# Attention over pooled keys and two dense layers on one core: the kernel lists its own instructions and orders them

## The chip, the cores and the metric

The kernel runs on one core of a Trainium2 chip. The metric is the device time of one execution in microseconds; the median of 3 runs before the change is 1000.41 us. The engines are TensorE (PE, with its weight loads, PEld), VectorE (DVE), ScalarE (ACT), GpSimd (POOL) and SyncE (SP, which issues most loads). Each engine takes its own instructions strictly in the order in which they were emitted for it, and waits for the others by semaphores.

## The reference

Eight batches of 576 tokens, 8 heads of 64 columns. The keys and values of a head are averaged over windows of 8, so that 72 are left; attention over them gives x of 4608 tokens by 512 columns, and two dense layers follow:

```python
k_p = k.reshape(B, H, 72, 8, 64).mean(axis=3)         # v_p in the same way
scores = np.matmul(q, k_p.transpose(0, 1, 3, 2)) / 8
attn = exp(scores - max); attn = attn / (sum + 1e-9)
x = np.matmul(attn, v_p)                              # to (4608, 512)
h = x @ w_in                                          # (512, 2048)
g = h * (1.0 / (1.0 + np.exp(-1.702 * h)))
out = g @ w_out                                       # (2048, 512)
```

The weights arrive as float64; q, k and v as float32.

## The kernel before

*Products.* An operand of float32 is split into hi, its rounding to 12 bits, and lo, the rest. A product is then three passes of the fast type: hi with hi, hi with lo, lo with hi. Lines 563 to 565 are the passes of `h` (w_in times x), lines 583 to 585 those of `o` (g times w_out). For a chunk of tokens `moe_in` computes h for one block of 128 of the 2048 columns (16 blocks, here called f = 0 to 15; for chunks of 256 tokens two blocks at once), ACT applies the gelu twice (line 569 gives gh, the hi part, 570 gives g), and line 572 subtracts to gl, the lo part, on DVE for the first two chunks and on POOL after that. `moe_out` adds the block to one accumulator of 128 tokens by 512 columns each, and after the last block ACT copies it out (588) and stores it (589). There are three chunks of 256 tokens and ten of 384.

*Weights.* The 33 parts of 512 (at the end 256) columns are turned from float64 to float32 by `decode_weights`: ACT 520 and 522, DVE 527 (shift) and 528 (merge), POOL 532, then ACT 538 writes the hi part and 543 the lo part, on POOL for three parts of four and on DVE for the fourth.

*Attention.* A batch's 576 tokens are two pieces of 256 and 320. Window sums of keys and values are made by `spread`: in the first batch by eight products with an identity on PE (line 142), in the others by a DVE reduction (147). Scores are float32 products (308), which take two instruction records each. DVE takes the maximum off (320, 321), ACT exponentiates (354), DVE sums (359) and multiplies by the inverse. In the first batch the multiply is wide (369), and PE turns the weights, tokens to keys (412). In the others 16 + 8 narrow multiplies a piece (389, 381) lay them out so that DVE can turn blocks of 32 (422, 437). The turned weights are split (ACT 425, DVE 426), multiplied with the values in four passes into `pav` (452 to 455), and split again into x (ACT 458, DVE 459). Pieces that reach over the end of a chunk leave a part in `stage`.

*Order.* `stream` is a generator of attention's stages. The main loop emits the products of one block of one chunk and then pulls stages out of the generator at a pace set by constants (`PACE`, `EARLY`, `DECODED`). The framework then reorders what was emitted, by a timeline simulation of its own (`schedule_with_timeline_sim`). x has two buffers, h two banks of PSUM, o three, attention three.

Of the kernel before, what the change touches and what calls it, by code (L numbers as in the profile page):

```python
# [19 lines left out]


@with_exitstack
def attention_moe_kernel(ctx: ExitStack, tc: tile.TileContext, q, k, v, w_in, w_out, out):
    """Every float32 product is three float32r passes: an operand x is hi + lo, hi the rounding of
    x to 12 significant bits and lo the exact rest, and hi*hi + hi*lo + lo*hi carries float32's bits."""
# [3 lines left out]
    NTOK = B * S  # L29
# [11 lines left out]
    # Tokens of a batch in two pieces, and each piece's tiles of tokens: first token and count.  # L41
# [3 lines left out]
    XBUFS = 2  # L45
    HEAD = 3
    CHUNK = 384
    OVER = 192  # tokens of a piece beyond its first chunk, at most
    AHEAD = 1
    PACE = 5  # L50
    EARLY = 13
    FETCHED = 1
    DECODED = 0.8
    LEAD = 4
    GAP = 2
    # The chunks of tokens of the second part: first token and count.
# [29 lines left out]
    x_tiles = {}  # L86

    def x_tile(c):
        if c not in x_tiles:
            x_tiles[c] = xpool.tile([P, 2, NJ, CHUNK], F32R, tag="x", name=f"x{c}")  # L90
        return x_tiles[c]

    def fetch_main(b, u, src, t=None):
        """Keys 0 to 63 of a pair's two heads in the two halves of the partitions."""
        if t is None:
            t = load.tile([P, NP, 512], F32, tag="kv", name=f"kv{b}_{u}_{src is v}")
        for a in range(2):
            ins = nc.sync.dma_start(
                out=t[a * KM : (a + 1) * KM],
                in_=src[b, UH * u + a : UH * (u + 1) : 2, 0 : KM * POOL].rearrange(  # L100
                    "j (p w) d -> p j (w d)", w=POOL
                ),
            )
            if b:
                tc.keep_in_program_order(ins)
        return t

    def fetch_tail(b, u, tl=None, copies=(v, v, v, k)):
        """The last keys of four heads: three copies of v's, and k's."""
        if tl is None:  # L110
            tl = load.tile([P, 512], F32, tag="tl", name=f"tl{b}_{u}")
        for r, src in enumerate(copies):
            if src is not None:
                nc.sync.dma_start(
                    out=tl[r * TAIL : (r + 1) * TAIL],
                    in_=src[b, UH * u : UH * (u + 1), KM * POOL :].rearrange("h (p w) d -> h p (w d)", w=POOL),
                )
        return tl

    def fetch_q(b, piece, j, place=None):  # L120
# [3 lines left out]
        qr = place  # L124
        if qr is None:
            qr = load.tile([P, PMAX // 32, 32], F32, tag="qr", name=f"qr{b}_{piece}_{j}", bufs=2)
        for a in range(2):
            for e in range(2):
                r = (2 * a + e) * 32
                nc.sync.dma_start(  # L130
                    out=qr[r : r + 32, 0 : npc // 32],
                    in_=q[b, 2 * j + a, o0 : o0 + npc, e * 32 : (e + 1) * 32].rearrange("(c i) d -> i c d", i=32),
                )
        return qr

    def spread(b, raw, bd, nm):
        """The window sums of 64 keys of each head, each pair's two heads on a block diagonal."""
        if b == 0:
            ps = ps_a.tile([P, 512], F32, tag="a", name=f"red{b}_{nm}")
            red = ps[:, 0 : NP * D].rearrange("p (i d) -> p i d", i=NP)  # L140
            for w in range(POOL):
                nc.tensor.matmul(
                    red, lhsT=ident, rhs=raw[:, :, w * D : (w + 1) * D], start=w == 0, stop=w == POOL - 1
                )
        else:
            red = att.tile([P, NP, D], F32, tag="red", name=f"red{b}_{nm}")
            nc.vector.tensor_reduce(  # L147
                out=red, in_=raw.rearrange("p i (w d) -> p i d w", w=POOL), axis=AX.X, op=ALU.add
            )
        nc.vector.tensor_tensor(  # L150
            out=bd,
            in0=red.unsqueeze(2).broadcast_to([P, NP, 2, D]),
            in1=mask2.unsqueeze(1).unsqueeze(3).broadcast_to([P, NP, 2, D]),
            op=ALU.mult,
        )
# [4 lines left out]
    batches = {}  # L160

    def fetch_batch(b):
        m = batches[b] = Batch()
        m.v = []
        m.k = [fetch_main(b, u, k) for u in range(NU)]
        m.tl = [fetch_tail(b, 0)]
        return m

    def fetch_first():
        """The first batch, where x and the last parts of the weights will lie; q as it is."""  # L170
        m = batches[0] = Batch()
        kt, vt = (xpool.tile([P, NU, NP, 512], F32, tag="x", name=f"{n}0") for n in "kv")
        m.k, m.v = [kt[:, u] for u in range(NU)], [vt[:, u] for u in range(NU)]
        tl = const.tile([P, NU, 512], F32, tag=f"w{2 * NF - 4}", name="tl0")
        m.tl = [tl[:, u] for u in range(NU)]
        whole, place = [], None

        def fetch_q_tile(i):
            nonlocal place
            s0, ns = (PIECES[0][1] + PIECES[1][1])[i]  # L180
            if i % 2 == 0:
                place = const.tile([P, 2, H, D], F32, tag=f"w{2 * NF - 1 - i // 2}", name=f"q0_{i // 2}")
            nc.sync.dma_start(out=place[:ns, i % 2], in_=q[0, :, s0 : s0 + ns].rearrange("h s d -> s h d"))  # L183
            whole.append(place[:ns, i % 2])
# [8 lines left out]
            "w": lambda: more_raws(len(raws) + 1),  # L193
# [497 lines left out]
```

## Time and profile before

| | us |
|---|---|
| three runs | 1000.41, 997.27, 1000.79 |
| median | 1000.41 |
| span of the profiled execution | 994.9 |
| PE, DVE, ACT, POOL busy | 939.4, 551.3, 411.9, 266.7 |
| mean granted clock of PE | 0.975 |

The profiled execution has no time of its own beside its span, which runs from the first to the last instruction; the median of the runs is 5.5 us above it. A row of a timeline is: start, length, engine, line, operation, result and operands, and in brackets the idle time before it and what ended that. A product's length includes the tail that overlaps the next product, so the pace is read from one start to the next. A row of groups ends with the count, the sum of busy time, the mean in ns, and the idle time ahead.

### The profile page before, as it was taken

Reading aid. Unit: us, or ns where it says so; the run is one execution under the profiler, and the core shown is the slowest. Engines: PE = TensorE matmul, PEld = TensorE weight load, DVE = VectorE, ACT = ScalarE, POOL = GpSimd, SP = SyncE. Lnnn points to the kernel's source line nnn. Section 1 sums busy time; section 2 is a strip of 40 time slices with the busy share of each in tenths; the row PEclk is TensorE's granted clock in tenths of the full one; section 3 lists DMA queues with packets and bytes.
Section 4 is the critical chain, followed back from the end, with each engine's and each line's share of the span. In section 5 each row is a group of like instructions: output and inputs, shape, how many; then the busy total and the mean of one; then the engine's idle time right before and its main releaser. Section 6 shows DMA issues by size and latency. Waiting matters only on the chain.

```text
span 994.9 us, 13412 instructions
## 1 busy us (share of the span) xinstructions
PE 939.4 (94%) x4957; PEld 835.0 (84%) x4957; DVE 551.3 (55%) x1094; ACT 411.9 (41%) x837; POOL 266.7 (27%) x240
## 2 busy tenths in 40 slices
PE   5597899989999999999989999999999999999998
PEld 4476698888878999899978989889988999999997
DVE  3999995789989660760788560680685410100000
ACT  3788553444336432452434342442445332322222
POOL 2568620111212222222212222222212322222222
PEclk8689799999999999999999999999999999999999
DMA  8984341312233030130223030130010000000000
GB/s 208 340 241 126 74 102 32 77 35 52 71 54 85 32 70 1 43 75 1 60 42 85 32 69 1 38 70 1 33 27 1 33 1 0 33 1 1 33 1 32
DMA packets 100449, 57.50 MB, mean 58 GB/s; under 512 B 75168, under 2 KB 83360, under 8 KB 100384
## 3 DMA queue, kind: packets, MB, share of 16 engines
q1 hardware_dynamic: 95200, 47.21, 19.6%
q10 hardware_dynamic: 5184, 9.44, 2.6%
q8 instruction: 39, 0.64, 0.3%
q14 instruction: 26, 0.21, 0.1%
HBM read 47.19 MB, written 9.44 MB: 57 GB/s over the span
## 4 chain that ended last, share of the span: by engine, by line
PE 63%; DVE 18%; DMA 6%; issue 4%; ACT 4%; SPq 3%; POOL 1%; DVEq 0%; ACTq 0%; POOLq 0%
PE h L565 10%; PE o L585 10%; PE h L564 10%; PE o L583 10%; PE h L563 10%; PE o L584 10%; DVE main L389 7%; DMA qr<-in_q_dram 2%; PE sps L308 2%; DMA tl<-in_v_dram 1%; DMA raw<-in_moe_w_out_dram 1%; SPq L183 1%; DVE al L426 1%; DVE tail L381 1%; DVE red_k L147 1%
## 5 line engine op out<-in xcount | busy, mean ns | idle before, releaser
L572 POOL TENSOR_TENSOR gl<-g,gh 128x384 fp32r<-128x384 f32 (+1 forms) x168 | 176.0, 1047 | 619.1 <-ACT g L570 595.6
L564 PE MATMUL h<-x,w 128*128 128x384 f32 (+1 forms) x832 | 274.0, 329 | 4.1 <-POOL w L543 3.5
L565 PE MATMUL h<-x,w 128*128 128x384 f32 (+1 forms) x832 | 273.5, 329 | 1.4 <-DVE x L459 1.4
L563 PE MATMUL h<-x,w 128*128 128x384 f32 (+1 forms) x832 | 273.6, 329 | 0.5 <-ACT x L458 0.4
L569 ACT ACTIVATE gh<-h 128x384 fp32r<-128x384 f32 (+1 forms) x184 | 93.0, 505 | 337.6 <-PE h L565 333.8
L583 PE MATMUL o<-w,gh 128*128 128x512 f32 x576 | 227.9, 396 | 2.6 <-ACT gh L569 2.5
L584 PE MATMUL o<-w,gh 128*128 128x512 f32 x576 | 227.8, 395 | 0.0
L585 PE MATMUL o<-w,gl 128*128 128x512 f32 x576 | 192.0, 399 | 3.3 <-DVE gl L572 3.0
L564 PEld LDWEIGHTS h<-x,w 128*128 128x128 f32 x832 | 160.2, 193 | 14.0 <-POOL w L543 4.1
L563 PEld LDWEIGHTS h<-x,w 128*128 128x128 f32 x832 | 159.9, 192 | 10.8 <-issue 0.8
L565 PEld LDWEIGHTS h<-x,w 128*128 128x128 f32 x832 | 159.2, 192 | 8.0 <-DVE x L459 1.6
L426 DVE TENSOR_TENSOR al<-mt,ah 128x256 fp32r<-128x256 f32 (+1 forms) x56 | 31.9, 569 | 180.1 <-PE pav L454 142.6
L583 PEld LDWEIGHTS o<-w,gh 128*128 128x128 f32 x576 | 108.7, 189 | 19.6 <-ACT gh L569 3.8
L585 PEld LDWEIGHTS o<-w,gl 128*128 128x128 f32 x576 | 106.2, 189 | 22.4 <-DVE gl L572 3.6
L584 PEld LDWEIGHTS o<-w,gh 128*128 128x128 f32 x576 | 108.8, 189 | 16.5 <-issue 0.4
L389 DVE TENSOR_TENSOR main<-sc,sm 32x256 f32<-32x256 f32 (+1 forms) x224 | 118.5, 529 | 3.2
L570 ACT ACTIVATE g<-h 128x384 f32<-128x384 f32 (+1 forms) x184 | 92.1, 501 | 13.8 <-DVE gl L572 6.9
L459 DVE TENSOR_TENSOR x<-pav,x 128x256 fp32r<-128x256 f32 (+3 forms) x64 | 24.9, 390 | 68.0 <-ACT x L458 67.9
L308 PE MATMUL sps<-k,qt 128*128 128x144 f32 (+1 forms) x320 | 57.6, 305 | 2.8 <-DVE sc L321 2.7
L308 PEld LDWEIGHTS sps<-k,qt 128*128 128x128 f32 (+1 forms) x320 | 45.4, 187 | 10.9 <-DVE sc L321 2.9
L532 POOL TENSOR_TENSOR raw<-raw 128x512 uint32<-128x512 uint32 (+1 forms) x33 | 41.5, 1261 | 40.8 <-DVE raw L528 14.5
L425 ACT CAST ah<-mt 128x256 fp32r<-128x256 f32 (+1 forms) x56 | 24.3, 434 | 52.9 <-DVE mt L422 39.6
(80 smaller groups left out, 891.7 us busy)
## 6 DMA issues: line engine op xcount, KB each, us to landing
out_dram<-osb ACTq DMA_DIRECT2D x36, 256.0 KB
raw<-in_moe_w_in_dram SPq DMA_DIRECT2D x16, 512.0 KB
raw<-in_moe_w_out_dram SPq DMA_DIRECT2D x15, 512.0 KB
kv_False<-in_k_dram SPq DMA_DIRECT2D x28, 256.0 KB
kv_True<-in_v_dram SPq DMA_DIRECT2D x28, 256.0 KB
qr<-in_q_dram SPq DMA_DIRECT2D x112, 40.0 KB
qr<-in_q_dram SPq DMA_DIRECT2D x112, 32.0 KB
tl<-in_v_dram SPq DMA_DIRECT2D x48, 64.0 KB
```

The source lines that it names most:

```text
L308: nc.tensor.matmul(ps[:ns, t * PW : (t + 1) * PW], lhsT=qt[:, s0 - o0 : s0 - o0 + ns], rhs=m.k2[:, j], start=True, stop=True,)
L389: nc.vector.tensor_tensor(out=main[32 * r : 32 * (r + 1), :, cols].rearrange("p j t k -> p t j k"), in0=sc[rows, 0:nt, a::2, 32 * half : 3 ...
L426: nc.vector.tensor_tensor(out=al[:, :npc], in0=pt[:, :npc], in1=ah[:, :npc].bitcast(F32), op=ALU.subtract)
L563: nc.tensor.matmul(o, lhsT=w[:, 0, j], rhs=x[:, 0, j], start=j == 0, stop=False)
L564: nc.tensor.matmul(o, lhsT=w[:, 1, j], rhs=x[:, 0, j], start=False, stop=False)
L565: nc.tensor.matmul(o, lhsT=w[:, 0, j], rhs=x[:, 1, j], start=False, stop=j == NJ - 1)
L569: nc.scalar.activation(out=gh, in_=h, func=AF.Gelu_apprx_sigmoid)
L570: nc.scalar.activation(out=g, in_=h, func=AF.Gelu_apprx_sigmoid)
L572: (nc.vector if c < 2 else nc.gpsimd).tensor_tensor(out=gl, in0=g, in1=gh.bitcast(F32), op=ALU.subtract)
L583: nc.tensor.matmul(o, lhsT=gh[:, i, tok], rhs=w[:, 0], start=f == 0, stop=False)
L584: nc.tensor.matmul(o, lhsT=gh[:, i, tok], rhs=w[:, 1], start=False, stop=False)
L585: nc.tensor.matmul(o, lhsT=gl[:, i, tok], rhs=w[:, 0], start=False, stop=f == NF - 1)
```

## The change

`Plan` is a list of tasks, each with an engine, a duration, a due time, the buffers that it reads and writes, and a function that emits it. `order` walks through time: whenever an engine is free, it takes among the tasks whose inputs are there (a fixed waiting time after the task that made them) and whose buffers have room the one with the earliest due time. The result is emitted task by task, and the framework's reordering is switched off (`manual_schedule`). Durations are linear in the size, with constants per engine; a change of ACT's function table adds 1.28, DVE and POOL at work together take 1.3 and 1.2 times as long, PE 1.5 times in the first 60 us.

With it go other edits. A chunk is now the first 512 tokens of a batch, and the ninth chunk gathers the last 64 tokens of all eight batches, which go through a buffer in DRAM; the first chunk is computed as two halves of 256 tokens, the second two blocks behind the first. The second batch is handled like the first (`TURNED = 2`): window sums, and turns of the attention weights, on PE, with wide multiplies on DVE. Each batch's value product has its lo pass last of the four. gl is on DVE only for the first 12 blocks of chunk 0. o has four banks, attention two. Two of a chunk's four outgoing tiles use the buffer of g, two the other one.

```diff
-    CHUNK = 384
-    AHEAD = 1
-    PACE = 5
+    CHUNK = 512
+    HALF = CHUNK // 2
+    LAG = 2
+    TURNED = 2
...
-    ps_o = ctx.enter_context(tc.tile_pool(name="ps_o", bufs=3, space=PSUM))
+    ps_o = ctx.enter_context(tc.tile_pool(name="ps_o", bufs=4, space=PSUM))
-    ps_a = ctx.enter_context(tc.tile_pool(name="ps_a", bufs=3, space=PSUM))
+    ps_a = ctx.enter_context(tc.tile_pool(name="ps_a", bufs=2, space=PSUM))
...
+    def order(self, log=None):
...
+                for t in ready[e]:
+                    if t.ready <= now + 1e-9 and (best is None or (t.due, t.k) < (best.due, best.k)) and self.room(t):
+                        best = t
...
+        if b < TURNED:
+            red = buf(ps_h if b == 0 else ps_a, [P, 512], F32, "h" if b == 0 else "a", f"red{b}_{nm}")
...
+                nc.tensor.matmul(o, lhsT=m.vt()[:96, j], rhs=at()[:96, :npc], start=False, stop=False)
+                nc.tensor.matmul(o, lhsT=m.vh()[:, j], rhs=al()[:, :npc], start=False, stop=True)
...
+                lambda: nc.sync.dma_start(out=left_dram[:, :, b * LEFT : (b + 1) * LEFT], in_=left()),
...
+        if c == 0 and fs[0] < 12:
+            dve(512, lambda: rest(nc.vector), [g, gh], [gl])
+        else:
+            pool(512, lambda: rest(nc.gpsimd), [g, gh], [gl])
...
+    FIRST, STEP, ROUND = 44.0, 6.0, 96.0
...
-        for what in "w k0 w k1 tk tv q q v0 v1 w w w w w w w w q q q".split():
+        for n, what in enumerate("w k0 k1 tk tv q q v0 v1 w w w w w q w q w q".split()):
...
+    for i in range(NF // 2):
+        dense(0, 0, HALF, (2 * i, 2 * i + 1), acc, FIRST + STEP * 2 * i)
+    for i in range(NF // 2):
+        dense(0, HALF, HALF, (2 * i, 2 * i + 1), acc, FIRST + STEP * (2 * i + LAG))
+    for c in range(1, B + 1):
+        acc = {}
+        for f in range(NF):
+            dense(c, 0, CHUNK, (f,), acc, FIRST + STEP * (NF + LAG) + ROUND * (c - 1) + ROUND * f / NF)
+
+    order = plan.order()
+    with tc.manual_schedule():
+        for t in order:
+            t.emit()
```

How it moves instructions, at three places. A row is the line, the operation, the result and its operands, and the shape; a name such as `sc1_0` is batch and piece, `h0_256_2` chunk, first token and block. First DVE, in the first piece of the second batch, from the sum of the exponentials on. Before:

```order
L359 TENSOR_REDUCE sm1_0_994<-sc1_0_992 128x16
L360 TENSOR_SCALAR sm1_0_994<-sm1_0_994 128x16
L363 RECIPROCAL sm1_0_994<-sm1_0_994 128x16
L381 TENSOR_TENSOR tail1_0_1120<-sc1_0_992,sm1_0_994 32x2x32 x2
L389 TENSOR_TENSOR main1_0_1119<-sc1_0_992,sm1_0_994 32x2x4x32 x4
L381 TENSOR_TENSOR tail1_0_1120<-sc1_0_992,sm1_0_994 32x2x32 x2
L389 TENSOR_TENSOR main1_0_1119<-sc1_0_992,sm1_0_994 32x2x4x32 x4
```

and two more such pairs. Now, with decoding of the last weights and the lo parts of the first chunk behind it:

```order
L554 TENSOR_REDUCE sm1_0_1345<-sc1_0_1237 128x16
L566 TENSOR_SCALAR sm1_0_1345<-sm1_0_1345 128x16
L569 RECIPROCAL sm1_0_1345<-sm1_0_1345 128x16
L582 TENSOR_TENSOR tail1_0_1378<-sc1_0_1237,sm1_0_1345 128x128
L582 TENSOR_TENSOR main1_0_1386<-sc1_0_1237,sm1_0_1345 128x1024
L452 TENSOR_TENSOR vl1_1399<-vbd1_1284,vh1_1347 128x512
L873 TENSOR_TENSOR w0_15_1357<-raws_681,w0_15_1357 128x512
```

Twenty-four multiplies became two, and the turns that followed on DVE are gone from it. Second, PE where the first dense products begin. Before, two blocks in turn while the first piece's values are still being made:

```order
L455 MATMUL pav0_0_0_471<-at0_0_0_454,vt0_426 128x256
L412 MATMUL apt0_0_1_490<-ident_79,main0_0_358 128x128 x2
L563 MATMUL h0_0_598<-x0_476,w0_0_177 128x256
L564 MATMUL h0_0_598<-x0_476,w0_0_177 128x256
L563 MATMUL h0_2_837<-x0_476,w0_2_237 128x256
L564 MATMUL h0_2_837<-x0_476,w0_2_237 128x256
L565 MATMUL h0_0_598<-x0_476,w0_0_177 128x256
```

Now, there, the three passes of one block:

```order
L717 MATMUL pav0_0_1_390<-al0_0_1_371,vh0_263 128x256
L639 MATMUL apt0_0_2_400<-ident_79,main0_0_315 128x128 x2
L639 MATMUL apt0_0_3_405<-ident_79,main0_0_315 128x128 x2
L509 MATMUL sps0_1_2_410<-k20_167,qt0_1_2_386 128x144 x2
L509 MATMUL sps0_1_2_410<-k20_167,qt0_1_2_386 64x144
L893 MATMUL h0_0_0_422<-x0_397,w0_0_128 128x256
L894 MATMUL h0_0_0_422<-x0_397,w0_0_128 128x256
L895 MATMUL h0_0_0_422<-x0_397,w0_0_128 128x256
L714 MATMUL pav0_0_2_429<-ah0_0_2_408,vh0_263 128x256
```

And the place further on at which the second half of the tokens (`h0_256_0`) starts, between the last value products of the second piece and the first half's block 5:

```order
L895 MATMUL h0_256_0_686<-x0_397,w0_0_128 128x256
L639 MATMUL apt0_1_3_699<-ident_79,main0_1_563 128x128 x2
L639 MATMUL apt0_1_3_699<-ident_79,main0_1_563 128x64
L714 MATMUL pav0_1_2_706<-ah0_1_2_679,vh0_263 128x320
L715 MATMUL pav0_1_2_706<-ah0_1_2_679,vl0_273 128x320
L716 MATMUL pav0_1_2_706<-at0_1_1_583,vt0_158 128x320
L717 MATMUL pav0_1_2_706<-al0_1_2_691,vh0_263 128x320
L893 MATMUL h0_256_0_686<-x0_397,w0_0_128 128x256
L894 MATMUL h0_256_0_686<-x0_397,w0_0_128 128x256
L895 MATMUL h0_256_0_686<-x0_397,w0_0_128 128x256
L893 MATMUL h0_0_4_577<-x0_397,w0_5_683 128x256
```

Every product of one block stands with its three passes together, both halves of the first 512 tokens use a block's weights shortly after each other, and the lo pass of `pav` has moved from third to last. Third, ACT at the exponentials of a later batch, before and now:

```order
L354 ACT_TABLE_LOAD
L354 ACTIVATE sc4_0_3423<-sc4_0_3423 128x1152
L569 ACT_TABLE_LOAD
L569 ACTIVATE gh1152_5_3636<-h1152_5_3622 128x384
L570 ACTIVATE g1152_5_3635<-h1152_5_3622 128x384
```

```order
L548 ACT_TABLE_LOAD
L548 ACTIVATE sc3_0_2891<-sc3_0_2891 128x1152
L908 ACT_TABLE_LOAD
L908 ACTIVATE gh2_0_2_2996<-h2_0_2_2920 128x512
L914 ACTIVATE g2_0_2_3015<-h2_0_2_2920 128x512
```

The group is the same; on PE, 27 products of h (blocks 3, 4 and a part of 5) stand now between the end of `h2_0_2` and the first product that reads `gh2_0_2`. On SP, the store of a batch's left-over tokens stands ahead of or among the loads of the next batch.

More of the change, by code (lines that the diff above doesn't have):

```diff
@@ L19, with __init__, __call__ @@
 POOL = 8
+ENGINES = ("DMA", "ACT", "DVE", "POOL", "PE")
+class Ring:
+    def __init__(self, room, fifo=False):
+        self.room, self.fifo, self.queue = room, fifo, []
+class Buf:
+    def __init__(self, ring, make, name=""):
+        self.name = name
+        self.ring, self.make, self.tile = ring, make, None
+        self.writes, self.reads, self.users, self.held = [], [], 0, False
+        if ring is not None and ring.fifo:
+            ring.queue.append(self)
+    def __call__(self):
+        if self.tile is None:
+            self.tile = self.make()
+        return self.tile
@@ L28, in attention_moe_kernel @@
     DM, DF = w_in.shape
-    NTOK = B * S
     KEYS = S // POOL
@@ L129, in fetch_q @@
                 r = (2 * a + e) * 32
[L130 to L154 removed]
+                dma(
+                    32 * npc * 4,
+                    lambda r=r, a=a, e=e: nc.sync.dma_start(
+                        out=qr()[r : r + 32, 0 : npc // 32],
+                        in_=q[b, 2 * j + a, o0 : o0 + npc, e * 32 : (e + 1) * 32].rearrange("(c i) d -> i c d", i=32),
+                    ),
+                    writes=[qr],
+                    run=128,
+                )
@@ new lines, in gather_left @@
+    def gather_left(c):
+        x = x_buf(c)
+        dma(
+            P * NJ * CHUNK * 4,
+            lambda: nc.sync.dma_start(out=x()[:, 1].bitcast(F32), in_=left_dram),
+            [left_refs],
+            [x],
+        )
+        for j in range(NJ):
+            act(
+                CHUNK,
+                lambda j=j: nc.scalar.copy(out=x()[:, 0, j], in_=x()[:, 1, j].bitcast(F32)),
+                [],
+                [(x, (0, 0, j))],
+            )
+            dve(
+                CHUNK,
+                lambda j=j: nc.vector.tensor_tensor(
+                    out=x()[:, 1, j], in0=x()[:, 1, j].bitcast(F32), in1=x()[:, 0, j].bitcast(F32), op=ALU.subtract
+                ),
+                [(x, (0, 0, j))],
+                [(x, (1, 0, j))],
+            )
@@ L178, in fetch_q_tile @@
         def fetch_q_tile(i):
[L179 to L184, printed above, removed]
+            s0, ns = tiles[i]
+            part = Part(places[i // 2], i % 2, lambda t: t[:ns, i % 2])
@@ L186, in fetch_first @@
+            dma(
+                ns * H * D * 4,
+                lambda: nc.sync.dma_start(out=part(), in_=q[0, :, s0 : s0 + ns].rearrange("h s d -> s h d")),
+                writes=[ref(part)],
+                run=256,
+            )
+            whole.append(part)
         todo = {
@@ L659, in attention_moe_kernel @@
-    for p in pending:
-        moe_out(*p)
+        return m, whole[:2], whole[2:]
+    m, *whole_q = first_batch()
+    plan.due = 10.0
+    sum_keys(0, m)
+    for piece in range(2):
+        plan.due = (14.0, 30.0)[piece]
+        held = scores(0, piece, m, whole_q[piece])
+        if piece == 0:
+            plan.due = 16.0
+            sum_values(0, m)
+        plan.due = (20.0, 45.0)[piece]
+        weigh(0, piece, m, *held)
+    for i in range(len(parts)):
+        if i not in raws:
+            plan.due = 10.0 + 3.0 * i
+            fetch_weights(i)
+        plan.due = 15.0 + 3.0 * i
+        decode(i)
@@ new lines, in attention_moe_kernel @@
+    for b in range(1, B):
+        m = Batch()
+        m.k = m.v = m.tl = None
+        start = FIRST + STEP * (NF + LAG) + ROUND * (b - 2) if b > 1 else 90.0
+        plan.start = start - 15
+        plan.due = start
+        sum_keys(b, m)
+        plan.due = start + 5
+        held = scores(b, 0, m)
+        sum_values(b, m)
+        plan.due = start + 15
+        weigh(b, 0, m, *held)
+        plan.due = start + 20
+        held = scores(b, 1, m)
+        plan.due = start + 30
+        weigh(b, 1, m, *held)
```

1148 lines of the change are left out of this document (699 added, 449 removed).

## The prediction

> **What bounds the kernel now.** I read the page first, then the windows of the first 140 us, then PE's timeline for the paces, and last the groups of DVE.
>
> ```profile
> span 994.9 us, 13412 instructions
> PE 939.4 (94%) x4957; PEld 835.0 (84%) x4957; DVE 551.3 (55%) x1094; ACT 411.9 (41%) x837; POOL 266.7 (27%) x240
> ...
> 0.00:20.00 20.00, 7.77 (x42) 6.49 (x43) 7.32 (x15) 5.93 (x10) 5.32 (x10) 0.93 0.75 187
> 20.00:40.00 20.00, 10.68 (x59) 8.79 (x59) 16.86 (x29) 14.38 (x28) 7.62 (x6) 0.76 1.04 313
> 40.00:60.00 20.00, 15.62 (x62) 12.28 (x63) 19.70 (x30) 15.65 (x32) 14.91 (x13) 0.59 1.03 317
> 60.00:80.00 20.00, 20.00 (x119) 17.01 (x118) 19.97 (x32) 16.86 (x28) 11.79 (x9) 0.96 0.83 259
> 80.00:100.00 20.00, 14.02 (x71) 10.94 (x69) 19.97 (x28) 16.73 (x31) 19.33 (x11) 0.91 0.29 62
> 100.00:120.00 20.00, 16.29 (x72) 13.42 (x73) 19.84 (x28) 11.23 (x24) 12.15 (x10) 0.74 0.29 68
> 120.00:140.00 20.00, 19.69 (x132) 17.88 (x131) 19.66 (x33) 12.65 (x26) 10.93 (x10) 1.00 0.43 88
> ```
>
> In each window the busy times are those of PE, its weight loads, DVE, ACT and POOL, then the granted clock. PE is busy for 94% of the whole, but until 120 us it is often idle or slow, while DVE is busy from 25 us to 140 us almost without a break. So the start is bound by DVE and the rest by PE. How much PE loses follows from the work that it has, at the pace of products that follow each other without a wait (starts of instructions):
>
> ```profile
> 909.38 0.34 PE L565 MATMUL h<-x,w 128*128 128x384 f32 x1
> 911.12 0.39 PE L583 MATMUL o<-w,gh 128*128 128x512 f32 x1
> ...
> 906.96 0.39 PE L583 MATMUL o<-w,gh 128*128 128x512 f32 x1
> 908.11 0.39 PE L584 MATMUL o<-w,gh 128*128 128x512 f32 x1
> ...
> 164.83 0.28 PE L565 MATMUL h<-x,w 128*128 128x256 f32 x1
> 165.55 0.28 PE L565 MATMUL h<-x,w 128*128 128x256 f32 x1
> ...
> 498.83 0.76 PE L308 MATMUL sps<-k,qt 128*128 128x144 f32 x4
> 499.33 0.43 PE L564 MATMUL h<-x,w 128*128 128x384 f32 x1
> ...
> 500.24 0.31 PE L453 MATMUL pav<-ah,vl 128*128 128x320 f32 x1
> 500.39 0.31 PE L454 MATMUL pav<-al,vh 128*128 128x320 f32 x1
> ...
> 335.98 0.39 PE L585 MATMUL o<-w,gl 128*128 128x512 f32 x1
> 989.44 0.85 PE L585 MATMUL o<-w,gl 128*128 128x512 f32 x3
> ```
>
> Ten products of 384 columns take 1.74 us, five of 512 take 1.15, six of 256 take 0.72: 0.174, 0.230 and 0.120 us each. A score product of 144 columns is two records of 0.125, a value product of 320 columns 0.15. The kernel has 1920, 1728 and 576 of the first three: 334 + 397 + 69 = 800 us. Scores (160 x 0.25 = 40), values (128 x 0.12 + 128 x 0.15 = 35) and some 17 us of window sums and turns make 892. PE's last product ends at 990.3, so 98 us are lost. Of the work, 253 us stand ahead of the product at 335.98 in PE's order (69 + 35 us of h, 99 of o, 50 of attention). So 83 us were lost before 336.4, and only 654 - 639 = 15 afterwards. Whatever the change gains must come out of those 83.
>
> **The change, part by part.** *Chunks.* Dense products become 1536 x 0.230 + 384 x 0.120 + 1728 x 0.230 = 797 us: 4 us less. *Second batch on TensorE.* PE gets four window sums of 8 products (two records of 0.12 each: 7.5 us) and 25 turns.
>
> ```profile
> 111.39 0.93 PE L412 MATMUL apt<-ident,main 128*128 128x128 f32 x3
> 118.33 0.59 PE L412 MATMUL apt<-ident,main 128*128 128x128 f32 x3
> ```
>
> At full clock (the second row) three turns are busy for 0.59 us, the first row has them at the low clock. A product's record runs on after the next one has started, by 0.28 - 0.12 = 0.16 us in the rows of 256 columns. So three turns cost 0.43 and 25 cost 3.6 us. PE's sum is then 892 - 4 + 7.5 + 3.6 = 899 us. The Trainium skill (TensorE: Matmul & The Clock Gate, section Part 4: PE-mode transpose) puts a turn on PE at about 275 ns within a kernel. By that the turns would be 7 us and the end 3 us later; the rows here show half of it, and I go by them. What DVE is spared:
>
> ```profile
> L389 DVE TENSOR_TENSOR main<-sc,sm 32x256 f32<-32x256 f32 (+1 forms) x224 | 118.5, 529 | 3.2
> L147 DVE TENSOR_REDUCE red_k<-kv_False 128x128 f32<-128x1024 f32 x14 | 27.8, 1984 | 5.0 <-DMA kv_False<-in_k_dram 5.0
> L369 DVE TENSOR_TENSOR main<-sc,sm 128x1024 f32<-128x1024 f32 x2 | 2.4, 1209 | 0.0
> L369 DVE TENSOR_TENSOR tail<-sc,sm 128x128 f32<-128x128 f32 x2 | 1.6, 823 | 0.0
> ```
>
> A batch's main multiplies are 118.5 / 7 = 16.9 us and its four sums 4 x 1.98 = 7.9; of the new form, three wide and three narrow multiplies cost at most 6 x 1.2. At least 17 us of DVE go from the second batch, in the stretch in which DVE is full.
>
> *The new order of the start.* Its price is the time at which PE comes to the first product that needs the sixth block of w_in (first half, f = 5), as from there it has the second half of the tokens to work on as well. DVE has 101 instructions up to that weight's low part. Bounds for when it is through:
>
> ```profile
> 0.00:80.00 80.00, 54.06 (x279) 44.58 (x279) 63.84 (x104) 52.82 (x95) 39.64 (x36) 0.81 0.91 269
> ...
> L528 DVE SCALAR_TENSOR_TENSOR raw<-raw,e 128x512 uint32<-128x512 uint32 x31 | 31.4, 1011 | 0.4
> L527 DVE TENSOR_SCALAR e<-e 128x512 uint32<-128x512 uint32 x31 | 18.9, 611 | 6.8 <-ACT e L520 6.8
> L543 DVE TENSOR_TENSOR w<-raw,w 128x512 fp32r<-128x512 f32 x8 | 7.4, 927 | 0.1
> ```
>
> DVE was idle for 12.7 + 3.1 = 15.8 us in the first 40, when data had not landed; k, q and v are loaded first in both, so I keep that. At the mean of the first 80 us (63.84 / 104 = 0.61) 101 instructions are 62 us: 78. By kind, 13 pairs of decoding (1.62) and 3 low parts (0.93) are 24 us and the softmax and splits of the first batch about 30: 70. On PE's side, the first half of x needs 63 of DVE's instructions, 15.8 + 31 = 47 us by kind, and then come 16.2 us of products. At the clock of the window from 40 to 60, 0.59, they take 27: 74. I take 75.
>
> ```profile
> 53.38 0.64 PE L289 MATMUL qps<-ident,q 128*128 128x128 f32 x3 [1.43 <-DVE x L459]
> 57.68 0.41 PE L563 MATMUL h<-x,w 128*128 128x256 f32 x1
> 57.89 0.41 PE L564 MATMUL h<-x,w 128*128 128x256 f32 x1
> ```
>
> The low clock is the pace of 0.21 us for 256 columns, four us behind a wait of 1.43. The Trainium skill (the same page, section Part 1: The HAM clock gate) says that the clock is halved only after an idle window of about 3.4 us. By that PE would be through its 16.2 us at 63, DVE's 70 would set the time, and the end would come 5 us earlier, which is what the first rival supposes. The rows show PE slow behind a wait of 1.43, so I keep 75.
>
> From the mark 866 us of the work remain: 941. Until the last x of batch 1, DVE's and PE's sums now run side by side: DVE has some 153 us by kind, less a tenth since its spans overlap (its means add to 136 until 140 us where 123 are busy), plus 15.8, which is 155; PE has 75 + 98 = 173 there. DVE is ahead by up to 18 us, and this cover hides the decoding and the second batch's loads; a microsecond by which it is overdrawn costs one. On SP's queue these loads now stand behind the store of the first batch's left-over tokens, which waits for the last value product of that batch, near 85 us; they hold up batch 1 alone, which has until 173. I put 3.5 us for switches between kinds of products in this stretch (below). *The rounds.* PE's loss behind 336 us, 15 us for 4.3 batches of attention, holds few waits:
>
> ```profile
> PE pav L454 <- DVE al L426: 4.2, 4, 1.5
> ```
>
> The rest, 2.4 us a batch, is switching (after four score records at 498.83 the next product of 384 takes 0.27 us instead of 0.174). Six batches lie behind the mark's stretch: 14, and 2 for waits, since the product that needs DVE's low part is now last of four: 16; the bounds are 8 and 21. The left-over tokens of the later batches go out by SP ahead of the next batch's last loads, which are needed a chunk later, and all come back at once during chunk 7, whose 88 us hide the load and its eight short conversions; without that cover they are some 8 us. Two of a chunk's four stores share a buffer, so the third copy waits for the first store: covered by the next chunk's first products, and at the end 0 to 4 us (the 4.6 below hold one such store), of which I take 1.
>
> **The sum.** 75 + 866 + 3.5 + 16 = 960.5, and 4.6 from PE's last product to the end as now, and 1: a span of 966. The median of the runs shown is 1000.41 for a profiled span of 994.9, so 5.5 are added: 971.5, and with the DVE end (70 instead of 75) counted for a third, 970. Within 0.5%, or 5 us, is the least that a measurement of this kernel can tell from no change.
>
> **Rivals.** *The halves mesh at once*: DVE's 70 us hold, the clock comes up as PE gets its backlog, and switches cost their lower end: 70 + 866 + 2 + 8 + 5 + 5.5 = 956, and 945 if the 15.8 idle us shrink as well. For it: DVE's sum is 9 to 18 us ahead of PE's behind 75 us. Against it: DVE, ACT and PE are all nearly full until 170 us, and each keeps its order, so a slip of one is handed on to the others.
>
> *The fixed order waits at the table switches.* ACT must stand at the exponentials until DVE has the scores, and behind them stand the gelus that PE waits for.
>
> ```profile
> 501.38 1.28 ACT L354 ACT_TABLE_LOAD   x1
> 505.76 1.17 ACT L354 ACTIVATE sc<-sc 128x1152 f32<-128x1152 f32 x1 [3.10 <-DVE sc L321]
> 507.15 1.28 ACT L569 ACT_TABLE_LOAD   x1
> 508.45 0.49 ACT L569 ACTIVATE gh<-h 128x384 fp32r<-128x384 f32 x1
> ```
>
> Such a visit took 7 us. In the new order 27 products, 6.2 us, stand between the end of h and the product that needs its gelu, which needs 0.6 more, and its low part 2: each of 12 visits could cost 0 to 2.5 us. 970 plus 12 to 30 is 982 to 1000.
>
> *The start stays slow (this is the slower one).* PE has 114 us of work from its first h to the last value product of batch 1. If each piece of it waits for decoding, the clock stays where 40 to 60 and 100 to 120 had it. At 0.74 that work takes 40 us more, which makes 1010; at 0.59, 79 more, which makes 1049. It decides below 0.77. For it: those windows had such waits, and PE now has more to do there. Against it: 60 to 80 had 0.96, and DVE has 17 us less to do.
>
> *It changes nothing*: the work differs by 7 us, and if losses stay at 98 the time is 1007. The orders shown differ, so this is unlikely.
>
> **How the numbers follow.** Forecast 0.61 (950 to 985), meshing 0.14, table switches 0.13, slow start 0.10, nothing 0.02. Faster: 0.61 + 0.14 + 0.10 + 0.02 = 0.87; the same: 0.03 of the switches, 0.02 of the start, 0.01; slower: 0.06 of the start and 0.01. The range from 945 to 995 leaves out the slow start but for its mildest form (0.08), the upper end of the switches (0.03), no change (0.02) and some meshing better than 945 (0.04), somewhat under 2 in 10.
>
> **What would show it.** The first 512 tokens were copied out by 194 us before:
>
> ```profile
> 193.36 0.59 ACT L588 COPY osb<-o 128x512 f32<-128x512 f32 x1 [0.18 <-PE o L585]
> ```
>
> Right: now they are near 180, the clock is above 0.9 from 75 us on, and chunks follow at 98 to 101 us with attention and 88 to 90 without. Wrong: windows between 80 and 160 with a clock under 0.8; PE waiting for gelus more than 10 us in all behind 200; DVE idle for more than 10 us between 40 and 150.

## The result, and the profile after

The changed kernel takes 977.2 us (median of 4 runs, 973.84 to 977.78), the kernel before 999.1 in the same comparison: a ratio of 0.977, with a 95% interval from 0.974 to 0.980. The forecast was 970.0. The profiled span is 975.2 us, 2.0 under the median.

The page of the changed kernel, and the windows of its first 140 us (columns as in the prediction):

```profile
span 975.2 us, 12254 instructions
PE 933.1 (96%) x4470; PEld 771.5 (79%) x4470; DVE 551.7 (57%) x1038; ACT 394.0 (40%) x745; POOL 246.7 (25%) x196
PEclk8689999999999999999999999999999999999998
```

```profile
0.00:20.00 20.00, 9.18 (x42) 8.11 (x43) 6.09 (x13) 5.24 (x9) 3.03 (x8) 0.92 0.76 179
20.00:40.00 20.00, 11.06 (x63) 9.65 (x64) 15.84 (x26) 12.60 (x22) 8.19 (x7) 0.67 1.09 322
40.00:60.00 20.00, 18.59 (x101) 14.85 (x100) 16.17 (x38) 12.62 (x27) 5.79 (x6) 0.73 1.06 376
60.00:80.00 20.00, 15.33 (x79) 12.13 (x80) 19.72 (x31) 16.38 (x36) 11.74 (x9) 0.83 0.44 154
80.00:100.00 20.00, 18.11 (x104) 14.89 (x103) 19.79 (x22) 15.15 (x27) 14.68 (x11) 1.00 0.30 70
100.00:120.00 20.00, 17.02 (x117) 15.38 (x116) 19.87 (x25) 15.52 (x28) 16.54 (x12) 0.98 0.20 43
120.00:140.00 20.00, 18.87 (x127) 17.52 (x127) 18.59 (x30) 13.62 (x22) 10.94 (x9) 0.94 0.39 80
```

Up to 80 us little is better than before. From 80 to 140 PE's clock is nearly whole (it was 0.91, 0.74 and 1.00), and PE is busier; DVE is as full as it was. Where the time went follows from PE's timeline: for each record, the time from its start to the next start, less the pace of its shape (the prediction's 0.120, 0.230, 0.150, 0.125 and so on). Summed by stretch, in us:

| stretch (before; after) | lost before | lost after |
|---|---|---|
| ahead of PE's first product | 7.7 | 7.3 |
| from there to 40 | 20.8 | 20.6 |
| 40 to 80; to 77 | 14.7 | 16.3 |
| 80 to 140; 77 to 140 | 19.9 | 9.3 |
| 140 to 194; to 192 (first 512 tokens done) | 5.0 | 3.1 |
| to 336 | 15.2 | 2.9 |
| to PE's last product | 15.7 | 11.7 |
| behind it | 4.6 | 6.6 |
| all; and the products themselves | 103.6; 891.3 | 77.8; 897.4 |

So 26 us less are lost and 6 more are worked. Most of the gain (22.9 of 25.8) lies in two stretches, 80 to 140 and 194 to 336. The waits of PE in the second one, before (a row ends with the us in total, the times and the longest):

```profile
PE sps L308 <- DVE sc L321: 2.7, 1, 2.7
PE pav L454 <- DVE al L426: 2.4, 3, 1.3
PE pav L452 <- DVE sc L321: 1.5, 1, 1.5
```

After the change this view of the same stretch has no row at all. In the first one, the longest before (80 to 140 us):

```profile
PE h L564 <- POOL w L543: 3.5, 2, 1.9
PE o L583 <- ACT gh L569: 1.8, 2, 1.5
PE pav L452 <- DVE al L426: 1.6, 1, 1.6
PE kps L230 <- DVE kbd L150: 1.6, 1, 1.6
```

And what is left (77 to 140 us, after):

```profile
PE kps L412 <- DVE kbd L364: 3.0, 1, 3.0
PE o L936 <- DVE gl L918: 1.4, 1, 1.4
PE red_v L344 <- DMA kv_True<-in_v_dram: 1.1, 1, 1.1
PE h L893 <- ACT g L914: 0.5, 1, 0.5
```

PE no longer waits for decoded weights (`w`), 4.3 us before in three rows, of which the first is shown. And by the windows of 20 us the clock that was withheld falls from 7.0 us (0.09 and 0.26 of 20) to 1.6 (0.02 and 0.06), an estimate of its share, as PE was not always busy then.

The place that the prediction calls the mark came at 76.79 us, and the last copy of the first 512 tokens at 192.35:

```profile
76.79 0.28 PE L893 MATMUL h<-x,w 128*128 128x256 f32 x1
...
192.35 0.58 ACT L946 COPY osb<-o 128x512 f32<-128x512 f32 x1 [0.73 <-PE o L936]
```

From there on a chunk with attention takes 99.2 to 99.8 us (first copies at 288.58, 388.35 and so on), one without 92.3 and 86.4. Between 60 and 125 us, DVE's groups by form (count, busy time, mean in ns, idle time) are these:

```profile
L853 DVE SCALAR_TENSOR_TENSOR raw<-raw,e 128x512 uint32<-128x512 uint32 x20 | 22.6, 1131 | 0.4
L846 DVE TENSOR_SCALAR e<-e 128x512 uint32<-128x512 uint32 x20 | 17.8, 891 | 0.0
L918 DVE TENSOR_TENSOR gl<-g,gh 128x512 fp32r<-128x512 f32 x8 | 8.5, 1063 | 0.0
```

49 of the 65 us are the decoding of weights and the lo part of the first chunk, not attention.

### The profile page after: what moved, and what is told of

It is laid out like the page before. It is cut to its first block, busy times and chain, and to the rows that moved or that the text cites. A ratio compares the mean times of both kernels' runs of the same rounds, so it can differ in the third digit from the quotient of the medians.

```text
span 975.2 us, 12254 instructions
## 1 busy us (share of the span) xinstructions
PE 933.1 (96%) x4470; PEld 771.5 (79%) x4470; DVE 551.7 (57%) x1038; ACT 394.0 (40%) x745; POOL 246.7 (25%) x196
## 4 chain that ended last, share of the span: by engine, by line
PE 85%; DVE 6%; issue 2%; DMA 2%; ACT 2%; SPq 1%; ACTq 1%; POOL 0%; POOLq 0%; DVEq 0%
PE h L893 13%; PE o L934 13%; PE h L894 13%; PE h L895 13%; PE o L935 12%; PE o L936 12%; PE sps L509 4%; DVE raw L853 2%; DVE e L846 1%; PE pav L714 1%; PE pav L716 1%; PE pav L717 1%; PE pav L715 1%; DMA raw<-in_moe_w_in_dram 1%; SPq L289 1%
## 5 line engine op out<-in xcount | busy, mean ns | idle before, releaser
L918 POOL TENSOR_TENSOR gl<-g,gh 128x512 fp32r<-128x512 f32 x132 | 172.8, 1309 | 644.3 <-ACT g L914 522.3
L893 PE MATMUL h<-x,w 128*128 128x512 f32 (+1 forms) x640 | 241.9, 378 | 1.8 <-ACT g L914 1.8
L894 PE MATMUL h<-x,w 128*128 128x512 f32 (+1 forms) x640 | 237.2, 371 | 0.0
L895 PE MATMUL h<-x,w 128*128 128x512 f32 (+1 forms) x640 | 237.0, 370 | 0.0
L936 PE MATMUL o<-w,gl 128*128 128x512 f32 x576 | 226.2, 393 | 2.5 <-DVE gl L918 1.4
L908 ACT ACTIVATE gh<-h 128x512 fp32r<-128x512 f32 x144 | 86.1, 598 | 303.0 <-PE h L895 270.9
L893 PEld LDWEIGHTS h<-x,w 128*128 128x128 f32 x640 | 121.9, 190 | 24.3 <-ACT g L914 2.7
L895 PEld LDWEIGHTS h<-x,w 128*128 128x128 f32 x640 | 121.8, 190 | 20.5
L894 PEld LDWEIGHTS h<-x,w 128*128 128x128 f32 x640 | 122.0, 191 | 18.6
L935 PEld LDWEIGHTS o<-w,gh 128*128 128x128 f32 x576 | 108.7, 189 | 20.6
L914 ACT ACTIVATE g<-h 128x512 f32<-128x512 f32 x144 | 85.4, 593 | 25.5 <-PE h L895 20.6
L498 DVE STREAM_TRANSPOSE qt<-qr 128x256 f32<-128x256 f32 (+1 forms) x56 | 25.8, 467 | 57.5 <-PE sps L509 55.8
L860 POOL TENSOR_TENSOR raw<-raw 128x512 uint32<-128x512 uint32 x30 | 35.1, 1169 | 59.5 <-DVE raw L853 48.1
L723 ACT CAST x<-pav 128x256 fp32r<-128x256 f32 x64 | 23.7, 371 | 46.6 <-PE pav L717 45.6
L527 DVE TENSOR_REDUCE nm<-sps 128x4 f32<-128x288 f32 x96 | 37.1, 387 | 6.6 <-PE sps L509 6.4
```

What stands on the lines that cost most here:

```text
L527: lambda ns=ns, g=g, hs=hs, view=view: nc.vector.tensor_reduce(out=nm()[:ns, g, hs], in_=view(), axis=AX.X, op=ALU.max, negate=True),
L893: nc.tensor.matmul(o, lhsT=w[:, 0, j], rhs=xs[:, 0, j], start=j == 0, stop=False)
L894: nc.tensor.matmul(o, lhsT=w[:, 1, j], rhs=xs[:, 0, j], start=False, stop=False)
L895: nc.tensor.matmul(o, lhsT=w[:, 0, j], rhs=xs[:, 1, j], start=False, stop=j == NJ - 1)
L908: lambda: nc.scalar.activation(out=gh(), in_=h(), func=AF.Gelu_apprx_sigmoid),
L914: 512, lambda: nc.scalar.activation(out=g(), in_=h(), func=AF.Gelu_apprx_sigmoid), [h], [g], table="gelu"
```

## The experiments

Two theories at first (the rivals *P*, *C* and *M* in the expectations are explained there). *D*: DVE's load in the front is what counts, and the second batch on PE made the gain. *O*: the order made it. Times are medians, beside 977.2 for the changed kernel and 998.5 to 1000.7 for the kernel before in the same comparisons; the intervals of the ratios to the latter are within 0.3% on each side, but for the framework's reordering (0.44%) and the last run without the maximum (0.35%).

**Second batch back on DVE, in the new order.**

```diff
-    TURNED = 2
+    TURNED = 1
```

> The changed kernel with the second batch treated like the later ones again (sums and turns on DVE, narrow multiplies). PE has 11.1 us less to do (7.5 + 3.6), DVE about 17.6 us more between 85 and 160 us. Theory D (DVE, full from 40 to 140 us, sets the time there and has no cover): slower by 10 to 18 us, 987 to 995; the last copy of chunk 0 moves from 192 to beyond 202. Rival O (the order alone made the gain, DVE has the cover of up to 18 us that I forecast): faster by 8 to 11 us for the work that PE is spared, 966 to 970.

1001.0 us, 24 slower than the changed kernel: rival O falls, and the price is above D's. PE, DVE and ACT in this kernel (the last number in brackets is the wait, and for whom):

```profile
152.26 0.80 PE L936 MATMUL o<-w,gl 128*128 128x512 f32 x1 [16.44 <-DVE gl L918]
```

```profile
138.31 1.50 DVE L602 TENSOR_TENSOR tail<-sc,sm 32x64 f32<-32x64 f32 x2
139.82 1.70 DVE L616 TENSOR_TENSOR main<-sc,sm 32x256 f32<-32x256 f32 x4
...
146.34 1.72 DVE L616 TENSOR_TENSOR main<-sc,sm 32x256 f32<-32x256 f32 x4
...
151.53 0.68 DVE L918 TENSOR_TENSOR gl<-g,gh 128x512 fp32r<-128x512 f32 x1
```

```profile
149.86 0.68 ACT L833 ACTIVATE e<-raws 128x512 f32<-128x512 f32 x1 [11.50 <-DVE raw L853]
```

Ten us of narrow multiplies stand in one piece in DVE's queue. PE waits for the `gl` behind them, and ACT for the decoding behind them. The list was planned anew, as in every run below that changes a task or a due time, so the 24 us hold the new order too.

**The same, with the second batch due later**, to see whether only the place was bad.

```diff
-        start = FIRST + STEP * (NF + LAG) + ROUND * (b - 2) if b > 1 else 90.0
+        start = FIRST + STEP * (NF + LAG) + ROUND * (b - 2) if b > 1 else 125.0
```

> The changed kernel with the second batch on DVE, as in an earlier run (1001 us), but its due time is 125 instead of 90, so that in DVE's order all lo parts of the first chunk (gl) stand ahead of its narrow multiplies. In that earlier run 10.5 us of narrow multiplies stood in one piece ahead of a gl for which PE waited 16.4 us. If the place in the fixed order made the loss: that wait goes, 983 to 990. If DVE's load made it: the wait only moves to another place, since the same multiplies then hold up the second batch's x: 995 to 1003.

1018.7 us, worse than either. The first 512 tokens are done at 172.3, 20 us sooner, but the second batch's x is not there, and PE has nothing else (its waits from 140 to 250 us):

```profile
PE kps L412 <- DVE kbd L364: 17.8, 2, 16.8
PE pav L714 <- ACT ah L700: 12.2, 2, 11.1
```

So the wait only moved: at neither of the two places did the load fit.

**Second batch on PE, in the old order** (the kernel before, `b == 0` made `b < 2` at its five places).

> The kernel before, with the second batch's window sums and turns on PE and wide multiplies on DVE, and nothing else changed. Theory D (DVE's load in the front is what counts, whatever the order): 17.6 us off DVE against 11 more on PE, faster by 3 to 10 us, 989 to 996. Rival O (without the new order it does not help): slower by 0 to 11 us, 999 to 1010.

1005.2 us, 0.6% slower than before (0.4 to 0.7%). With DVE relieved, PE still lost 22 us between 77 and 140, now by waits for ACT above all: 6.0 us for one `ah`, 4.1 for two `gh`. Neither part alone gains anything ("new" holds all the other edits, the chunks of 512 and the banks among them):

| | second batch on DVE | on PE |
|---|---|---|
| old kernel and order | 1000 | 1005 |
| new list and order | 1001 | 977 |

**The new list, reordered by the framework.**

```diff
-    with tc.manual_schedule():
-        for t in order:
-            t.emit()
+    for t in order:
+        t.emit()
```

> The changed kernel's instructions, emitted in the same sequence, but with the framework's own reordering switched on again. Rival O (the order made the gain): the losses behind 192 us come back, 15 us of them in the stretch from 192 to 336 as before the change, and some in front: 990 to 1002. Theory D (the gain is the work taken from DVE in the front, whatever the order): within 5 us of the changed kernel, 972 to 982.

1044.5 us: 67 slower, more than O expected. Losses come back behind 77 us: 19 us between 77 and 100 alone, some 23 between 192 and 336 (2.9 with the fixed order), 40 between 336 and 890 (8.5). The first row of PE's waits over the whole run is one that the fixed order hardly has, with one wait of 3.3 to 4.1 us in each of the four rounds from 340 us on:

```profile
PE sps L509 <- DVE sc L535: 16.0, 6, 4.1
```

**Twice the merge** of decoding for the parts from the 17th on.

```diff
+        for again in range(2 if i >= 16 else 1):
             dve(n, lambda: nc.vector.scalar_tensor_tensor(out=hi(), in0=hi(), scalar=0x80000000, ...
```

> The merge of decoding (DVE, 1.06 us in the mean) is done twice for the parts from the 17th on; the second one changes nothing in the value. That is 17 more instructions and, at 0.69 to 1.44 us each, 12 to 24 us more on DVE between 78 and 143 us, and nothing more on any other engine. Theory D (no cover left on DVE): slower by 10 to 20 us, 987 to 997. Rival C (the cover of up to 18 us of my forecast is there): slower by 0 to 4 us, 977 to 981.

991.9 us: 14.7 slower for 16.1 us more of merging on DVE (50.0 us in 50 instructions, 33.9 in 33 without). PE's waits for DVE from 77 to 192 us, 4.4 in the changed kernel, grow to 11.4, with these two rows ahead:

```profile
PE o L937 <- DVE gl L919: 4.2, 3, 1.8
PE tpt L639 <- DVE tail L582: 4.0, 1, 4.0
```

So the cover of 18 us was not there. How much of the 14.7 us is the load and how much the order isn't shown: with more tasks the planner moved PE's instructions too, from the 347th on.

**Less work for DVE.** If DVE's load in the whole front sets the time, taking some away must gain. First the maximum and its subtraction in the first two batches (left out; ACT copies the scores), then the window sums of the last keys and values on PE.

```diff
+                if b < TURNED:
+                    act(nt * PW, lambda ...: nc.scalar.copy(out=sc()[:ns, g, hs], in_=view()), [ps], [(sc, ns)])
+                    continue
```

> The changed kernel without the subtraction of the maximum in the first two batches (part of the computation is left out there): ACT copies the scores out of PSUM instead. DVE has 2 x (16 x 0.44 + 8 x 0.30), 19 us, less between 25 and 160 us, ACT some 9 more. Theory D (DVE sets the time in the front, at the 0.87 us for a us that doubling the merge showed): faster by 10 to 16 us, 961 to 967. Rival P (PE itself comes next, since only 6.7 us of its waits stand behind 76.8 us): faster by 4 to 8 us, 969 to 973.

```diff
+            if b < TURNED:
+                tred = buf(ps_h if b == 0 else ps_a, [P, 512], F32, "h" if b == 0 else "a", f"tred{b}_{u}")
...
+                pe(2 * POOL * 60, windows, [ref(tl)], [tred], also=[m.tbd])
```

> The changed kernel with the sums over the windows of the last keys and values of the first two batches (four reductions of 128x512 on DVE, 1.07 us each) as products on PE as well. DVE has 4.3 us less, PE some 2 more. Theory D: faster by 2 to 4 us, 973 to 975. Rival P (PE's backlog sets the time): slower by 0 to 2 us, 977 to 979.

983.5 and 993.7 us: both slower, by 6 and 16, and theory D as I had it falls. In both, the planner had made a new order. In the first the losses up to 192 us hardly change, and in the rounds PE now waits 7.2 us in all for ACT's copies of finished tiles, 0.4 with the old plan. In the second PE waits 8.8 us for `gl` and the clock falls behind it; PE also has more to do than the 2 us expected, 64 records of 0.112 us or 7.2, so its 16 us are not the order's alone. That called for a run in which the order stays.

**Less work for DVE, order kept.** The maximum is left out where the tasks are emitted, not where they are planned; PE's instructions stand in the same order as in the changed kernel.

```diff
-                    lambda ...: nc.vector.tensor_reduce(
+                    lambda ...: b < TURNED or nc.vector.tensor_reduce(
...
-                    lambda ...: nc.vector.tensor_tensor(
+                    lambda ...: nc.scalar.copy(out=sc()[:ns, g, hs], in_=view()) if b < TURNED else nc.vector.tensor_tensor(
```

> The changed kernel's order kept as it is on PE, POOL and for all that stays on DVE and ACT; only the maximum and its subtraction in the first two batches are left out (part of the computation is missing there), and ACT copies the scores out of PSUM at the place of the subtraction. DVE has 19 us less until 160 us, ACT some 9 more. Without the maximum but with an order planned anew, the kernel took 983.5 us. If that loss came from the new order (theory O, the order's details weigh as much as DVE's load) and DVE's load bounds the front: faster than the changed kernel, 962 to 971. If DVE's load ahead of 60 us is hidden behind the loads of the weights, and only what lies between 78 and 143 us counts: 970 to 976. If the load does not count at all: 976 to 985.

975.9 us (972.4 to 979.1), no different from 977.2. Without the maximum, the new order thus cost 7.6 us by itself. And 19 us less for DVE give nothing, in this order, with some 8 us more for ACT until 200 us (the copies). The windows show why:

```profile
40.00:60.00 20.00, 17.45 (x99) 14.04 (x98) 11.65 (x20) 14.99 (x34) 6.85 (x6) 0.79 1.06 375
60.00:80.00 20.00, 16.83 (x83) 13.63 (x84) 19.72 (x34) 16.59 (x37) 11.28 (x10) 0.83 0.45 159
80.00:100.00 20.00, 18.09 (x107) 15.05 (x107) 19.79 (x21) 15.15 (x27) 14.43 (x12) 1.00 0.30 73
100.00:120.00 20.00, 17.04 (x120) 15.40 (x119) 19.87 (x23) 15.32 (x28) 17.15 (x12) 1.00 0.20 41
```

DVE falls from 16.2 to 11.7 us between 40 and 60, where it had room already, and from 60 to 120 us it is as full as with the maximum: in the changed kernel the 48 instructions left out stand from 24 to 57 us and from 125 to 165, none in between. So this run shows that load outside that stretch does not count in this order; what less load inside it would give, no run shows. PE stops at the same places for as long: 4.59 us for a `tail` at 62.65 (4.42 at 63.59 in the changed kernel), 3.0 for `kbd`, 1.4 for `gl`.

**The first chunk in one piece.**

```diff
-    for i in range(NF // 2):
-        dense(0, 0, HALF, (2 * i, 2 * i + 1), acc, FIRST + STEP * 2 * i)
-    for i in range(NF // 2):
-        dense(0, HALF, HALF, (2 * i, 2 * i + 1), acc, FIRST + STEP * (2 * i + LAG))
+    for f in range(NF):
+        dense(0, 0, CHUNK, (f,), acc, FIRST + STEP * f)
```

> The changed kernel with its first chunk as one piece of 512 tokens, like the others. PE then gets its first dense product only with the second half of x (near 75 us where it was 50), and 16.2 us of products between them move behind it; 192 pairs of 0.1197 become 192 of 0.2295, 1.9 us less. Theory D (DVE's queue sets the time until 140 us, and PE catches up beside it): slower by 0 to 6 us, 975 to 983. Rival P (PE's backlog from 75 us on sets it): slower by 12 to 16 us, 989 to 993.

989.8 us, 12.6 slower, as rival P had it: PE's first dense product comes at 71.9 instead of 50.2, and PE is idle for 13.7 us between 40 and 77 where it was idle for 6.1.

**The lo pass third of four again.**

```diff
+                nc.tensor.matmul(o, lhsT=m.vh()[:, j], rhs=al()[:, :npc], start=False, stop=False)
-                nc.tensor.matmul(o, lhsT=m.vt()[:96, j], rhs=at()[:96, :npc], start=False, stop=False)
-                nc.tensor.matmul(o, lhsT=m.vh()[:, j], rhs=al()[:, :npc], start=False, stop=True)
+                nc.tensor.matmul(o, lhsT=m.vt()[:96, j], rhs=at()[:96, :npc], start=False, stop=True)
```

> The changed kernel with the lo pass of the value product third of four again, as before the change. The product that needs DVE's low part is met one product, 0.12 to 0.15 us, earlier, 64 times. If its place is what took the 6.6 us of PE's waits for al out of the rounds: slower by 3 to 7 us, 980 to 984. If the order of the whole list did it: within 2 us, 975 to 979.

975.3 us: its interval (0.974 to 0.978) lies over that of the changed kernel, so its place is worth nothing that can be measured. Beside it only the run without the maximum came out lower (975.9), so no version beats the changed kernel by more than its uncertainty.

**Earlier loads, and a shorter end.** ACT issues the first batch's tails and values, which the planner counts as free. In a second run ACT and DVE also copy the last four tiles in turn, and SP stores them.

```diff
+        for n, what in enumerate("tk tv v0 v1".split()):
+            plan.due = -200.0 + n
+            early.append(nc.scalar)
...
-        for n, what in enumerate("w k0 k1 tk tv q q v0 v1 w w w w w q w q w q".split()):
+        for n, what in enumerate("w k0 k1 q q w w w w w q w q w q".split()):
```

> The changed kernel, with the first batch's tails and values (12 loads, 11.6 us of issuing on SP's queue) issued by ACT, which has nothing to do from 8.6 to 16.9 us, and the three last tiles of q one weight earlier. The weights' loads then start some 10 us earlier than at 16.8 us. Theory D (DVE sets the time until 140 us, and it was idle for 14 of the first 20 us for want of data): faster by 5 to 10 us, 967 to 972. Rival M (the transfers themselves are full from 20 to 60 us, so that the order of issue changes nothing): within 2 us, 975 to 979.

> The kernel of the run before this one, and the last chunk's four tiles copied out by ACT and DVE in turn into a buffer of x that is free by then, and stored by SP instead of ACT. PE's last product is now followed by 2.8 us of copies and stores that ACT still has to issue and 3.8 for the last to land; the first of these should nearly go: faster than the run before by 1.5 to 3 us.

988.7 us and, with the end changed too, 988.5: slower than either theory of the first run had it. I had taken SP's issuing for the limit, and the loads did not land sooner. DVE, in the first of the two:

```profile
13.57 1.04 DVE L390 TENSOR_REDUCE tred<-tl 128x64 f32<-128x512 f32 x1 [11.44 <-DMA tl<-in_v_dram]
14.64 0.42 DVE L400 TENSOR_TENSOR tbd<-tred,mask 128x256 f32<-128x256 f32 x1
18.59 1.01 DVE L390 TENSOR_REDUCE tred<-tl 128x64 f32<-128x512 f32 x1 [3.52 <-DMA tl<-in_v_dram]
```

In the changed kernel these two sums start at 12.72 and 15.38. With two queues the tails came later, and DVE, whose order put them first, was busy for 3.7 us of the first 20 instead of 6.1. That the transfers are the limit is argued and not shown: this order is new as well, and while the first 512 tokens are done 5 us later (197.59), the other 5 us come behind that, where these loads have long landed. The end itself became 1.6 us shorter in the traces (from PE's last product on 8.0 us in the first run, 6.4 in the second, 6.6 in the changed kernel); the front of the second, 5 us later than that of the first in its profiled execution, hides that.

## Why the prediction was right in sign and 7 us off

- *The gain must come out of the 83 us ahead of 336.* So it did: 24 of 26 us. The work came out as summed (897 against 899).
- *The mark at 75.* 76.8. Neither of my two ends set it alone: DVE's softmax kept PE waiting for 4.42 us at 63.59, and the clock was low from 61.1 to 67.9.
- *From the mark to the last copy of the first 512 tokens, 3.5 us of loss.* 12.4: this is the step that failed ("DVE is ahead by up to 18 us, and this cover hides the decoding"). I compared the sums of DVE's and PE's work until 173 us (DVE's comes to 154 and not 155, which makes the cover larger still). What counts is what DVE has to do from 60 to 125 us, where decoding and the lo parts take 49 of 65: the doubled merge cost 14.7 us where the cover should have hidden it, and the run without the maximum in the kept order shows that DVE's spare time ahead of 60 and behind 125 cannot be used. So the copies came at 192 and not near 180. Of the 12.4 us, PE's waits for DVE are 4.4 and the low clock some 1.6; 1.6 more are waits for a load and a gelu, and the other 4.8 are not far from the 3.5 that I had for switches.
- *The second batch on PE*: 11 us of PE for 17 of DVE. The run shows 24 us in the new order (planned anew), as the multiplies held up ACT's decoding and PE's lo parts as well, and a small loss in the old one. I treated the parts as terms of a sum; they are conditions of each other.
- *The rounds, 16.* 14.6 behind 192 us, some 1.7 in a round of 100 us, with hardly a wait in it. PE waited for gelus 2.0 us in all behind 200, so the rival of the table switches falls. The lo pass, to which I gave some of it, does nothing.
- *The slow start.* Between 77 us and the last chunk the clock was low for only 3.4 us, at 119. The rival's place was right, though: the runs with a worse order or more load fell into it (a granted clock of 0.57 from 140 to 160 us with the second batch back on DVE).
- *It meshes at once*: 20 us too low, for the same cover (and its lower end, 956 less 15.8, is 940 and not 945).
- *The end*: 6.6 us behind the last product for 5.6, since each tile of the last chunk has two stores, and ACT issues them between its copies (the last product and the last copy):

```profile
967.96 0.63 PE L936 MATMUL o<-w,gl 128*128 128x512 f32 x1
...
970.82 0.58 ACT L946 COPY osb<-o 128x512 f32<-128x512 f32 x1 [1.25 <-issue]
```

- *Around the span*: 2.0 us, not 5.5; that hid part of the 9 us by which the span was longer than forecast, and this part is luck. The kernel before has only some 2.2 us around its span as well (998.15 for a span of 996.0, and so in all of its executions beside the experiments); the rest of the 5.5 was that its profiled execution was a quick one.
- *The signs*: a chunk with attention took 99.2 to 99.8 us, as forecast; one without 92.3 and 86.4, on either side of it; the clock was above 0.9 from 80 us on. But DVE was idle for 10.3 us between 40 and 150, just over what I had named as a sign of being wrong: 4.4 of it lie behind 140 and 3.8 ahead of 60, only 2.0 between.

Left open: what chunks of 512 tokens and the four banks of o give by themselves, what less load on DVE between 60 and 120 us would give in a kept order, and what the front would cost if DVE and POOL did not hold each other up (last section); none was tried.

## What to carry to other kernels

Where several engines are full at once, compare their sums stretch by stretch, not up to the end of the stage: spare time in one stretch does not help the next when each engine keeps a fixed order. A list ordered by hand or by a planner is good for the load that it was made for: an edit that takes work away can cost more by the new order than it saves (7.6 us in the one pair of runs that tells them apart), so keep the order fixed when you want to know what a load costs. And do one part of a change at a time in both directions: here the second batch on PE and all the rest were each worth nothing alone.

## What the runs showed of the hardware

*DVE and POOL.* The shift and the merge of decoding (`e`, `raw`) take 0.42 and 0.69 us when POOL is idle, and up to 1.53 when it is at work. DVE, then POOL, in the changed kernel:

```profile
98.25 0.42 DVE L846 TENSOR_SCALAR e<-e 128x512 uint32<-128x512 uint32 x1
98.71 1.41 DVE L853 SCALAR_TENSOR_TENSOR raw<-raw,e 128x512 uint32<-128x512 uint32 x1
...
102.43 1.53 DVE L846 TENSOR_SCALAR e<-e 128x512 uint32<-128x512 uint32 x1
103.88 1.06 DVE L388 TENSOR_REDUCE tred<-tl 128x64 f32<-128x512 f32 x1
```

```profile
98.47 1.10 POOL L860 TENSOR_TENSOR raw<-raw 128x512 uint32<-128x512 uint32 x1 [1.75 <-DVE raw L853]
...
101.92 3.21 POOL L873 TENSOR_TENSOR w<-raw,w 128x512 fp32r<-128x512 f32 x2
```

The merge at 98.71 ends 0.55 us behind POOL's instruction: it reads as a wait for it. The sum at 103.88, with one input, is as long as without POOL (1.03 at 12.72). Operations that read PSUM are not lengthened either (`sc` of 128x288 took 0.46 us at 24.74, with POOL idle, and at 29.96, beside it). From 60 to 125 us this comes to 21.6 us over `e`, `raw`, `gl` and `w` (busy time less 0.42 or 0.69 each). The planner takes 1.3 for every DVE operation beside POOL. The Trainium skill (SBUF — State Buffer, section Who interferes with whom) describes a port pair that DVE and GpSimd lock for a whole instruction when DVE has two inputs in SBUF or a two-port mode; the rows agree.

*The clock.* It changes at steps of 3.41 us. Windows laid on these steps (PE busy, loads, DVE, ACT, POOL, granted clock):

```profile
57.70:61.10 3.40, 1.47 (x13) 1.26 (x11) 3.30 (x5) 3.37 (x5) 2.29 (x2) 1.00 1.07 377
61.10:64.50 3.40, 0.91 (x4) 0.41 (x4) 3.33 (x7) 1.97 (x4) 1.29 (x1) 0.50 1.06 377
64.50:67.90 3.40, 3.40 (x14) 2.95 (x15) 3.32 (x7) 3.31 (x8) 1.35 (x1) 0.50 1.05 368
67.90:71.30 3.40, 3.40 (x19) 2.59 (x17) 3.33 (x6) 3.40 (x10) 2.23 (x3) 1.00 0.12 42
...
115.70:119.10 3.40, 0.45 (x3) 0.31 (x3) 3.37 (x5) 2.80 (x5) 3.40 (x3) 1.00 0.30 48
119.10:122.50 3.40, 3.40 (x16) 3.36 (x17) 3.33 (x3) 2.06 (x4) 3.11 (x3) 0.50 0.57 146
122.50:125.90 3.40, 3.40 (x28) 3.31 (x27) 3.37 (x6) 2.10 (x5) 1.72 (x2) 1.00 0.17 40
```

A step in which PE is busy for 0.45 or 1.47 of 3.4 us is followed by one at half the clock, and a full one restores it. So a wait of 2.98 us (ahead of `kps` at 118.65) costs another 1.6 in clock, by estimate from 3.4 us at 0.5. Where the limit lies is not shown: in the kernel before, a step with PE busy for 1.97 us (from 95.8) was followed by a full one, and the next, with 1.81, by one at half. The Trainium skill (TensorE: Matmul & The Clock Gate, Part 1: The HAM clock gate) lets the clock fall after an idle window; here PE was busy for 43% of the window ahead of 61.1 us, and it fell.
